# Unit 0's q and k through GpSimd's queue as bf16, turned without a copy

## The chip, the core and the metric

The kernel runs on one core of a Trainium2 chip. A core has TensorE (PE in the profile, PEld its weight loads), VectorE (DVE), ScalarE (ACT), GpSimd (POOL) and SyncE (SP), and sixteen DMA engines that move data between device memory and the on-chip memory. Every engine works through its own instruction list in order; semaphores make one wait for another. The metric is the device time of one execution in microseconds (us). Loads can be issued by SP and ACT (hardware_dynamic queues in the profile) or by GpSimd (software_dynamic queue); only the loads that GpSimd issues change the type on the way, here from float32 to bf16.

## The reference

Attention, then a two-layer block with a leaky ReLU, on float32 inputs:

```python
# q, k, v: (8, 12, 448, 64); w_in: (768, 2048); w_out: (2048, 768)
scores = np.matmul(q, k.transpose(0, 1, 3, 2)) / 8
attn = softmax(scores)                       # over the keys
x = np.matmul(attn, v)                       # heads side by side: (3584, 768)
h = x @ w_in
out = np.maximum(0.01 * h, h) @ w_out        # (3584, 768)
```

## The kernel before, in words

**Units.** A unit is a pair of heads of one batch entry, so there are 48, six to a batch entry. For a unit q and k come in as rows (112 partitions, four rows of 64 to a partition and head), are turned by TensorE or by a DMA transpose into `qkT` (128 partitions: the two heads' 64 components), and give scores in four chunks of 112 keys (`scores`, L331). ScalarE takes the exponential of each chunk from PSUM (`expo`, L349 to L351), TensorE multiplies it with v (`pv`, L360, and `rows`, L866), and VectorE divides by the sums (reciprocal L375 or L899, product L376 or L900) to give x, which is turned again and fed to the two-layer block in steps of 384 to 640 rows. Both layers use seven products in place of eight per pair of blocks; sums of weight blocks for this are made on VectorE (`mix_w_in`, L454, and `mix_weights`, L435).

**Order.** The schedule is written out by hand. Each engine executes in the order in which the code names its instructions; for the later stages a small model of due times (`place`, L973) chooses that order while the program is built. GpSimd's loads wait for the eighth load before them, so that at most eight are on their way.

**The start (L226 to L286).** SP and ACT load k and q of unit 0 as float32 (224 KB each), then k and q of unit 1; SP then loads v of unit 0. GpSimd makes the identity for the transposes, and then copies one column of unit 0's q (L234), which makes it wait for that load, before it issues its own loads: unit 2's q and k, v of units 1 and 2, unit 3's q and k, and so on (`load_soft`, L167). TensorE multiplies constants 39 times (`warm_up`, L271). VectorE clears small edges of tiles. ScalarE loads its table of functions behind its two load issues (L252). Then `both` (L281) casts k and q of unit 0 to bf16 in `qkb`, one head on ScalarE and one on VectorE.

**The first turn (`transposes`, L306).** For unit 0, k is turned first and q second, each by four transposes of 112 x 128 (both heads side by side), a few multiplications by zeros (`stay_warm`, L265: 3 behind k, 5 behind q), and a copy out of PSUM (k on ScalarE, q on VectorE, L320). The scores of unit 0 follow. Unit 1's k and q are cast on VectorE (L796) and turned behind the third chunk of unit 0.

**The second place (`neck`, L703).** While the first layer's columns beyond the head are made (L716), VectorE makes the sums of w_out's quarters, step by step, where `after` (L722) says: its tuple gives the number of steps after each of the eight groups. There are two rounds of six sums (L442, L444, L447); the second round needs the last of w_out's four loads. In between stand the reciprocal and product of a unit's x (L899, L900), which free a PSUM slot of TensorE's scores. Behind the sums stand four subtractions in w_out itself (L451). The second layer (`block_pair`, L604) follows: after its first product VectorE subtracts blocks of h (L633) and copies the result out of PSUM (`keep`, L626), and the third product uses the summed weights `w_mix`.

Of the kernel before, what the change touches and what calls it, by code (L numbers as in the profile page):

```python
# [16 lines left out]
def kernel(  # L17
# [13 lines left out]
    P = 128  # L31
# [135 lines left out]
    def load_soft(u, n, which):  # L167
        b, hp = divmod(u, HP)
        for x in which:
            if x > 0 and u >= WIDE:  # L170
                load_wide(u, x)
                continue
            t = room(x)
            nc.gpsimd.dma_start(
                out=half(t)[:, :n].rearrange("p u h so d -> p (u h) (so d)"),
                in_=(q, k, v)[x][b, 2 * hp:2 * hp + 2 * n].rearrange(
                    "h (p so) d -> p h (so d)", so=NSC),
            )
            for i in range(n):
                raw.setdefault(u + i, {})[x] = half(t, i)  # L180

    def load_one(u, x, queue):
        b, hp = divmod(u, HP)
        t = room(x)[:SC]
        queue.dma_start(
            out=t.rearrange("p h so d -> p h (so d)"),
            in_=(q, k, v)[x][b, 2 * hp:2 * hp + 2].rearrange("h (p so) d -> p h (so d)", so=NSC),
        )
        raw.setdefault(u, {})[x] = t
# [33 lines left out]
                o, i = w_steps.pop(0)  # L223
                nc.gpsimd.dma_start(out=o, in_=i)  # L224

    load_one(0, 1, nc.sync)  # L226
    load_one(0, 0, nc.scalar)
    load_one(1, 1, nc.sync)
    load_one(1, 0, nc.scalar)
    early = c_pool.tile([P, 4 * P], F32, name="c")  # L230
    ident = early[:, :P // 2].bitcast(BF16)
    make_identity(nc, ident)
    load_one(0, 2, nc.sync)
    nc.gpsimd.tensor_copy(early[:SC, P // 2 + 2:P // 2 + 3], raw[0][0][:, 0, 0, :1])  # L234
    load_soft(2, 1, (0, 1))
    load_soft(1, 2, (2,))
    load_soft(3, 1, (0, 1))
    cast(0, (2,))
# [8 lines left out]
    nc.vector.memset(warm[:, :P], 0.0)  # L247
    nc.vector.memset(warm[:, P:], 0.0)

    gate = early[:, P // 2:P // 2 + 2]  # L250
    nc.vector.memset(gate, 0.0)
    nc.scalar.copy(gate[:, :1], gate[:, 1:])  # L252

    ones = nc.const_aps.tensor(1.0, [P, P], BF16)

# [12 lines left out]
        for _ in range(n):  # L268
            nc.tensor.matmul(ps[:, 0, :P], warm[:, :P], warm[:, :P], start=True, stop=True)

    warm_up(39)  # L271
    for t in v_sb:
        nc.vector.memset(t[:, :, :, D:D + 1], 1.0)
    for t in e_sb:
# [2 lines left out]
    for t in qkT:  # L277
        nc.vector.memset(t[:, QL:QL + P - SC], 0.0)
    fast = nc.vector.tensor_copy

    def both(o, i):  # L281
        nc.scalar.copy(o[:, 0], i[:, 0])
        fast(o[:, 1], i[:, 1])

    cast(0, (1,), both)
    cast(0, (0,), both)  # L286


    x_t = {}
# [16 lines left out]
    def transposes(u, bank=None):  # L306
        if u >= min(NPE, NU):
            return
        gone.add(u)
        for parts in ((1,), (0,)) if u == 0 else ((0, 1),):  # L310
            tr = turn_tile(bank)
            for i in parts:
                for so in range(NSC):
                    nc.tensor.transpose(
                        tr[:, i, ts(so, SC)], qk_sb[u][:SC, i * NSC + so], ident[:SC, :SC]
                    )
            if u == 0:
                stay_warm(3 if parts == (1,) else 5)
            at = slice(parts[0], parts[-1] + 1)
            (nc.scalar.copy if u == NPE - 1 or u == 0 and parts == (1,) else nc.vector.tensor_copy)(  # L320
                qkT[u % NQ][:, :QL].rearrange("p (i s) -> p i s", i=2)[:, at], tr[:, at]
            )
# [281 lines left out]
    def block_pair(i, c):  # L604

        lo, hi = slice(0, MH), slice(MH, MD)
        x1, x2 = spots(i)[1][c]
        one, two = ts(x1, P), ts(x2, P)
        s3 = h_mix[:, :, c]
        t2, t3, t4 = (w_mix[:, x] for x in range(3))  # L610
        t1 = w_out_sb[:, lo, NW:]
        left, right = slice(0, NW), slice(NW, DM)
        o1 = o_pool.tile([P, DM], F32, name="o")
        o2 = o_pool.tile([P, DM], F32, name="o")
        b, a = banks

        def product(ps, x, w, first=False, cols=slice(0, NW)):
            for m in range(MH):
                if m in (2, 4, 6):
                    yield  # L620
                nc.tensor.matmul(  # L621
                    ps[:, cols], x[:, m], w[:, m], start=(first and m == 0), stop=(m == MH - 1), skip_group_check=True,
                )

        def keep(o, at, ps, by=nc.vector.tensor_copy):
            by(o[:, at], ps[:, :NW])  # L626

        def join(o, at, ps):
            nc.vector.tensor_add(o[:, at], o[:, at], ps[:, :NW])  # L629

        yield
        yield from product(b, h[:, lo, one], w_out_sb[:, lo, left], first=True)
        nc.vector.tensor_sub(h[:, lo, one], h[:, lo, two], h[:, lo, one])  # L633
        short = cuts[i + 1] - cuts[i] < 4 * P
        keep(o1, left, b, nc.scalar.copy if c == 0 and (short or i + 1 == NR) else nc.vector.tensor_copy)
        yield
        yield from product(a, h[:, hi, one], w_out_sb[:, hi, left], first=True)
        join(o1, left, a)
        nc.vector.tensor_sub(h[:, hi, one], h[:, hi, one], h[:, lo, one])
        yield  # L640
        yield from product(b, h[:, lo, one], t2)
        keep(o1, right, b)
        yield
        yield from product(a, h[:, lo, two], t1, first=True)
        keep(o2, right, a)
        yield
        yield from product(b, s3, t3)
        join(o2, right, b)
        yield
        t0 = token(i, x2)  # L650
        last = t0 + P == B * S
        if last:
            nc.vector.tensor_copy(o2[:, 2 * P:NW], b[:, 2 * P:NW])
            store(o1, token(i, x1), left)
            store(o2, t0, right)
        yield from product(a, h[:, hi, one], w_out_sb[:, hi, right])
        join(o1, right, a)
        if last:
            store(o1, token(i, x1), right, (nc.sync, nc.scalar))
        else:  # L660
            store(o1, token(i, x1))
        yield
        if last:
            w1, w2 = slice(0, 2 * P), slice(2 * P, NW)
            yield from product(b, h[:, hi, two], t4[:, :, w1], cols=w1)
            nc.vector.tensor_copy(o2[:, w1], b[:, w1])
            store(o2, t0, w1, (nc.scalar, nc.sync))
            end = slots[0][:, 0]
            yield from product(end, h[:, hi, two], t4[:, :, w2], first=True, cols=w2)
            nc.vector.tensor_add(o2[:, w2], o2[:, w2], end[:, w2])  # L670
            store(o2, t0, w2, (nc.sync, nc.scalar))
            return
        yield from product(b, h[:, hi, two], t4)
        keep(o2, left, b)
        store(o2, t0)
        banks.reverse()

    known = slice(0, HEAD - 3 * P)
# [24 lines left out]
    def neck(outs):  # L703

        n = cuts[1] - HEAD
        at = place_of(HEAD)
        ms = [x + y for x in range(0, MH, 2) for y in (0, MH)]
        held = {}

        def part2(m, kks):  # L710
            fresh = m not in held
            if fresh:
                held[m] = next_bank()
            for j in range(2):
                for kk in kks:
                    nc.tensor.matmul(  # L716
                        held[m][:, j * n:(j + 1) * n], w_in_sb[:, kk, ts(m + j, P)], xT[:, kk, at:at + n],
                        start=(fresh and j == 0 and kk == 0), stop=(kk == KD - 1), skip_group_check=True,
                    )

        assert all(u == need[1] - 1 for u, _ in owed_x), owed_x
        def after(x):  # L722
            for _ in range((0, 0, 2, 3, 4, 3, 0, 3)[x]):
                next(outs)

        for m in ms[:2]:
            part2(m, range(KD - 1))
        yield 4 * (KD - 1) * n / 2400, False
        for x, m in enumerate(ms):
            if x < 2:  # L730
                assert rows_done >= need[1], rows_done
                settle_x()
                part2(m, (KD - 1,))
                if x:
                    after(x - 1)
            else:
                part2(m, range(KH))
                after(x - 1)
                yield 2 * KH * n / 2400, False
                part2(m, range(KH, KD))  # L740
            nc.scalar.activation(
                h[:, m:m + 2, HEAD:cuts[1]], held.pop(m)[:, :2 * n].rearrange("p (m t) -> p m t", m=2), AX.Prelu, alpha=0.01
            )
            if x < 2:
                mix_first(4 * x, 1, known)
                mix_first(4 * x + 2, 1, known)
            settle(1)
            yield 2 * (KH if x > 1 else 1) * n / 2400, True
        model["free"][id(slots[0])] = model["now"] + 1.5
        transposes(NPE - 1, next_slot()[:, 0])  # L750
        after(len(ms) - 1)
# [388 lines left out]
```

## Time and profile before

| | |
|---|---|
| time, median of 3 runs | 380.48 us (380.31 to 380.56) |
| time of the profiled execution | 382.25 us |
| its span, first to last instruction | 380.1 us |
| PE busy | 372.1 us (98%) |
| ACT busy | 253.1 us (67%) |
| VectorE busy | 232.6 us (61%) |
| GpSimd busy | 153.4 us (40%) |
| first load of k landed, issued at 0.76 | 4.34 us |
| first load of q landed, issued at 0.76 | 4.70 us |
| GpSimd's first load issue | 5.00 us |
| first scores on PE | 6.66 us |
| first exponential on ACT | 7.06 us |
| last quarter of w_out landed | 70.90 us |

Times within the execution count from the start of the span. A line of a timeline reads: start, length, engine, line of the kernel, operation, output<-input, shapes, and xN for N such instructions together; in brackets stands how long the engine was idle before and what ended that. A line L12 is line 12 of the kernel; a helper's line stands for all its callers. Matmuls are pipelined, so one's length is longer than the distance to the next (its pitch). A DMA's time to landing counts from its issue.

### The profile page before, as it was taken

Reading aid. Unit: us, or ns where it says so; the run is one execution under the profiler, and the core shown is the slowest. Engines: PE = TensorE matmul, PEld = TensorE weight load, DVE = VectorE, ACT = ScalarE, POOL = GpSimd, SP = SyncE. Lnnn points to the kernel's source line nnn. Section 1 sums busy time; section 2 is a strip of 40 time slices with the busy share of each in tenths; the row PEclk is TensorE's granted clock in tenths of the full one; section 3 lists DMA queues with packets and bytes.
Section 4 is the critical chain, followed back from the end, with each engine's and each line's share of the span. In section 5 each row is a group of like instructions: output and inputs, shape, how many; then the busy total and the mean of one; then the engine's idle time right before and its main releaser. Section 6 shows DMA issues by size and latency. Waiting matters only on the chain.

```text
span 380.1 us, 9894 instructions
## 1 busy us (share of the span) xinstructions
PE 372.1 (98%) x3969; PEld 261.9 (69%) x3969; DVE 232.6 (61%) x512; ACT 253.1 (67%) x392; POOL 153.4 (40%) x302
## 2 busy tenths in 40 slices
PE   9899999899999999999999999999999999999995
PEld 7665658655598565896558975589755896668753
DVE  3662767687566655568475674655746566574753
ACT  5997895765777867677684786846867478318600
POOL 5866654397434934337333383334463000000000
PEclk9999999999999999999999999999999999999999
DMA  8999999999889997999957999679997550330022
GB/s 161 176 197 203 196 158 204 179 129 191 111 172 110 99 155 143 145 139 103 140 106 139 141 104 117 128 120 146 88 126 148 123 84 0 109 84 14 0 85 84
DMA packets 107678, 48.07 MB, mean 126 GB/s; under 512 B 79728, under 2 KB 104304, under 8 KB 107632
## 3 DMA queue, kind: packets, MB, share of 16 engines
q0 software_dynamic: 48096, 22.24, 51.1%
q1 hardware_dynamic: 58800, 24.54, 35.3%
q10 hardware_dynamic: 736, 0.66, 0.6%
q8 instruction: 31, 0.51, 0.6%
q14 instruction: 15, 0.12, 0.1%
HBM read 45.61 MB, written 11.01 MB: 149 GB/s over the span
## 4 chain that ended last, share of the span: by engine, by line
PE 78%; DMA 16%; POOL 3%; DVE 2%; issue 1%; POOLq 0%; DVEq 0%
PE g L621 34%; PE g L549 14%; PE sc L549 14%; PE sc L337 6%; DMA w_out_sb<-in_moe_w_out_dram 6%; PE sc L888 6%; DMA fq<-in_q_dram 4%; DMA w_mix<-in_v_dram 3%; PE sc L893 2%; PE sc L356 2%; DMA w_in_mix<-in_v_dram 1%; PE sc L877 1%; DMA hmix<-in_q_dram 1%; POOL w_in_sb L224 0%; POOL qkb L209 0%
## 5 line engine op out<-in xcount | busy, mean ns | idle before, releaser
L351 ACT ACTIVATE e<-sc 128x896 bf16<-128x896 f32 (+1 forms) x162 | 137.5, 922 | 43.5 <-PE sc L337 43.3
L621 PEld LDWEIGHTS <-h 128*128 128x128 bf16 x680 | 62.8, 98 | 50.1 <-issue 12.9
L621 PE MATMUL g<-w_out_sb,h 128*128 128x384 bf16 x448 | 86.4, 327 | 0.1
L538 ACT ACTIVATE h<-c 128x512 bf16<-128x512 f32 (+1 forms) x72 | 43.7, 611 | 28.2 <-DVE c L564 13.3
L549 PEld LDWEIGHTS <-w_in_sb 128*128 128x128 bf16 x576 | 54.6, 98 | 6.2
L337 PE MATMUL sc<-qkT 64*128 64x448 bf16 x324 | 42.5, 353 | 2.8 <-DVE x L900 1.4
L626 DVE COPY o<-g 128x384 f32<-128x384 f32 x53 | 29.4, 555 | 25.1 <-PE g L621 24.9
L549 PEld LDWEIGHTS <-w_in_mix 128*128 128x128 bf16 x432 | 41.0, 98 | 4.0
L209 POOL COPY v<-fv 128x256 f32<-128x256 f32 (+1 forms) x38 | 16.1, 433 | 67.7 <-PE sc L893 47.0
L621 PE MATMUL g<-w_mix,h 128*128 128x384 bf16 (+1 forms) x224 | 41.9, 325 | 0.0
L629 DVE TENSOR_TENSOR o<-o,g 128x384 f32<-128x384 f32 x42 | 23.2, 552 | 19.6 <-PE g L621 17.7
L888 PEld LDWEIGHTS <-e 128*128 128x128 bf16 x720 | 30.4, 97 | 3.5 <-ACT e L351 2.4
L888 PE MATMUL sc<-v,e 128*128 128x65 bf16 x720 | 32.1, 193 | 0.0
L209 POOL COPY qkb<-fq 112x256 f32<-112x256 f32 x38 | 16.7, 440 | 37.9 <-DMA qkT<-qkb 19.4
L900 DVE TENSOR_TENSOR x<-sc,rec 112x512 bf16<-112x512 f32 x42 | 29.0, 692 | 1.5
L337 PEld LDWEIGHTS <-qkT 64*128 64x128 bf16 x324 | 12.5, 94 | 25.1 <-issue 18.1
L549 PE MATMUL g<-xT,w_in_sb 128*128 128x256 bf16 (+1 forms) x216 | 28.5, 268 | 0.0
L549 PE MATMUL sc<-xT,w_in_sb 128*128 128x256 bf16 (+1 forms) x216 | 28.5, 268 | 0.0
L899 DVE RECIPROCAL rec<-sc 112x8 f32<-112x8 f32 x42 | 8.7, 207 | 29.5 <-PE sc L893 14.2
L893 PE MATMUL sc<-v,e 128*128 128x130 bf16 x120 | 26.7, 223 | 0.0
L209 POOL COPY qkb<-fk 128x256 f32<-128x256 f32 (+1 forms) x38 | 18.7, 492 | 19.0 <-DMA fk<-in_k_dram 17.9
L621 PE MATMUL g<-w_mix,hmix 128*128 128x384 bf16 x112 | 23.1, 326 | 0.0
(123 smaller groups left out, 589.5 us busy)
## 6 DMA issues: line engine op xcount, KB each, us to landing
fq<-in_q_dram POOLq DMA_DIRECT2D x19, 224.0 KB, 5.9
w_in_sb<-in_moe_w_in_dram POOLq DMA_DIRECT2D x4, 768.0 KB, 12.6
w_out_sb<-in_moe_w_out_dram POOLq DMA_DIRECT2D x4, 768.0 KB, 19.6
fk<-in_k_dram POOLq DMA_DIRECT2D x15, 192.0 KB, 5.7
fv<-in_v_dram POOLq DMA_DIRECT2D x15, 192.0 KB, 4.2
out_dram<-o SPq DMA_DIRECT2D x7, 336.0 KB, 3.6
out_dram<-o SPq DMA_DIRECT2D x8, 288.0 KB, 3.4
out_dram<-o SPq DMA_DIRECT2D x7, 240.0 KB, 3.1
```

Source lines behind the costliest of these rows:

```text
L209: by(t.rearrange("p so h d -> p h so d") if x < 2 else t[:, :, :, :d], f)
L337: nc.tensor.matmul(ps[:, j, :S], t[j * D:(j + 1) * D, k0:k0 + P], q_of(u)[j * D:(j + 1) * D] if u >= WIDE else t[j * D:(j + 1) * D, :S], s ...
L351: nc.scalar.activation(e[:, :, c, :], sc_t.pop((u, c))[:e.shape[0], :, :S], AX.Exp, scale=scale)
L538: nc.scalar.activation(hs[:, m:m + 2, cols], x.rearrange("p (m t) -> p m t", m=2), AX.Prelu, alpha=0.01)
L549: nc.tensor.matmul(ps[:, j * nh:(j + 1) * nh], w[:, kk, ts(j, P)], x[:, kk], start=(first and j == 0 and kk == 0), stop=(kk == KH - 1), sk ...
L621: nc.tensor.matmul(ps[:, cols], x[:, m], w[:, m], start=(first and m == 0), stop=(m == MH - 1), skip_group_check=True,)
L626: by(o[:, at], ps[:, :NW])
L629: nc.vector.tensor_add(o[:, at], o[:, at], ps[:, :NW])
L888: nc.tensor.matmul(ps[:, b, y + j, :D + 1], e[:, at:at + P], vt[:, j, c, :D + 1], start=(y + j + c == 0), stop=False, skip_group_check=True,)
L893: nc.tensor.matmul(ps[:, b, y:y + 2, :D + 1], e[:, at:at + P], vt[:, :, NWC, :D + 1], start=False, stop=True, skip_group_check=True,)
L899: nc.vector.reciprocal(rec, ps[:SC, :, :, D:D + 1])
L900: nc.vector.tensor_mul(x, ps[:SC, :, :, :D], rec.to_broadcast([SC, 2, NSC, D]))
```

## The change

Unit 0's k and q are loaded by GpSimd, as its first two instructions, as bf16. The transposes read the loaded rows directly: each head of each row group on its own (112 x 64), eight per tensor, into the upper or lower 64 partitions of PSUM. The casts of unit 0 and GpSimd's touch of q go. SP now loads only unit 1's k; unit 1's q and unit 0's v are issued by ACT, behind its table load, which moves ahead with the small memset that it reads. The warm-up goes from 39 to 29 multiplications, those behind k from 3 to 0 and behind q from 5 to 6. In `after` the counts for groups 4 to 6 go from 4, 3, 0 to 3, 0, 4, so that the six sums of the second round are split: two before, and four behind, the reciprocal and product of a unit's x. The order of all other instructions on the engines stays; `queues` in `block_pair` is given its default.

```diff
-    load_one(0, 1, nc.sync)
-    load_one(0, 0, nc.scalar)
+    load_soft(0, 1, (1, 0))
     load_one(1, 1, nc.sync)
-    load_one(1, 0, nc.scalar)
     early = c_pool.tile([P, 4 * P], F32, name="c")
+    gate = early[:, P // 2:P // 2 + 2]
+    nc.vector.memset(gate, 0.0)
+    nc.scalar.copy(gate[:, :1], gate[:, 1:])
     ident = early[:, :P // 2].bitcast(BF16)
     make_identity(nc, ident)
-    load_one(0, 2, nc.sync)
-    nc.gpsimd.tensor_copy(early[:SC, P // 2 + 2:P // 2 + 3], raw[0][0][:, 0, 0, :1])
     load_soft(2, 1, (0, 1))
+    load_one(1, 0, nc.scalar)
+    load_one(0, 2, nc.scalar)
     load_soft(1, 2, (2,))
...
-    gate = early[:, P // 2:P // 2 + 2]
-    nc.vector.memset(gate, 0.0)
-    nc.scalar.copy(gate[:, :1], gate[:, 1:])
...
-    warm_up(39)
+    warm_up(29)
...
-    def both(o, i):
-        nc.scalar.copy(o[:, 0], i[:, 0])
-        fast(o[:, 1], i[:, 1])
-
-    cast(0, (1,), both)
-    cast(0, (0,), both)
...
                 for so in range(NSC):
+                    if u == 0:
+                        for j in range(2):
+                            nc.tensor.transpose(tr[j * D:(j + 1) * D, i, ts(so, SC)], raw[0][i][:, j, so], ident[:SC, :SC])
+                        continue
                     nc.tensor.transpose(
                         tr[:, i, ts(so, SC)], qk_sb[u][:SC, i * NSC + so], ident[:SC, :SC]
                     )
             if u == 0:
-                stay_warm(3 if parts == (1,) else 5)
+                stay_warm(0 if parts == (1,) else 6)
...
-        store(o2, t0)
+        store(o2, t0, queues=(nc.sync, nc.sync))
...
-            for _ in range((0, 0, 2, 3, 4, 3, 0, 3)[x]):
+            for _ in range((0, 0, 2, 3, 3, 0, 4, 3)[x]):
```

## The prediction

> **What bounds the kernel now.** I read the page's busy times first, then the chain that ended last, then the waits stage by stage, then the timelines of the two places that the change touches. PE is busy for 98% of the span:
>
> ```profile
> PE 372.1 (98%) x3969; PEld 261.9 (69%) x3969; DVE 232.6 (61%) x512; ACT 253.1 (67%) x392; POOL 153.4 (40%) x302
> ```
>
> This is a mean over stages with different limits. The first is ScalarE's (its timeline, 0 to 40 us):
>
> ```profile
> 5.52 0.53 ACT L320 COPY qkT<-g 128x448 bf16<-128x448 bf16 x1 [0.40 <-PE g L314]
> 7.06 19.61 ACT L351 ACTIVATE e<-sc 112x896 bf16<-112x896 f32 x24 [1.01 <-PE sc L337]
> 27.12 2.53 ACT L351 ACTIVATE e<-sc 112x896 bf16<-112x896 f32 x3 [0.44 <-PE sc L337]
> ```
>
> 24 exponentials run without a pause from 7.06 to 26.67, 0.82 us each, so whatever moves the first one moves the stage. From 26 us PE is full, with one hole. The chain of waits from 0 to 80 us, whose columns are start, length and what, shows it behind a transfer:
>
> ```profile
> 48.38 22.53 DMA w_out_sb<-in_moe_w_out_dram
> ...
> 71.00 0.57 DVE w_mix L442
> ...
> 74.50 0.70 DVE x L900
> 75.20 0.04 issue
> 75.24 0.56 PE sc L337 x4
> ```
>
> The timelines of PE and VectorE show the same place from both sides:
>
> ```profile
> 73.48 0.36 PE L337 MATMUL sc<-qkT 64*128 64x448 bf16 x2
> 75.24 0.56 PE L337 MATMUL sc<-qkT 64*128 64x448 bf16 x4 [1.40 <-DVE x L900]
> ```
>
> ```profile
> 71.00 0.56 DVE L442 TENSOR_TENSOR w_mix<-w_out_sb 128x768 bf16<-128x768 bf16 x1 [3.31 <-DMA w_out_sb<-in_moe_w_out_dram]
> ...
> 73.13 1.22 DVE L447 TENSOR_TENSOR w_mix<-w_out_sb,w_mix 128x768 bf16<-128x768 bf16 x2
> 74.27 0.19 DVE L899 RECIPROCAL rec<-sc 112x8 f32<-112x8 f32 x1
> 74.50 0.69 DVE L900 TENSOR_TENSOR x<-sc,rec 112x512 bf16<-112x512 f32 x1
> ```
>
> VectorE waits 3.31 us for the last quarter of w_out (landed 70.90), does six sums for the weights, and only then empties the PSUM slot that PE filled by 71.5. PE stands 1.40 us for it. From 80 to 300 us it is idle for 0.1 us in all, so what PE wins here should reach the end.
>
> **Edit 1, the order on VectorE (tuple in `after`).** The counts of steps go from 2, 3, 4, 3, 0, 3 to 2, 3, 3, 0, 4, 3 (positions 2 to 7). In the changed order the reciprocal and x stand behind two of the six sums, not behind all six. With w_out at 70.90 again, the sums start at 71.00 and 71.59, the reciprocal at 72.06 (where the third sum was) and x at 72.29, done at 72.98. PE reaches its scores at 73.84: no stall, **1.40 us won**, 0.86 us to spare. What is late next: the four other sums take 2.21 us (72.06 to 74.27 before), so from 72.90 to 75.11; two of L451 follow as before to 76.12, the subtraction of L633 (pitch 0.61) to 76.73, the copy L626 (0.55) to 77.28. PE's first product with w_mix needs that copy, ran at 78.67, and now comes at 77.27. So this edit alone fits to 0.01 us, and what is won earlier passes only as far as w_out lands earlier too.
>
> **Edit 2, the start.** It removes two ScalarE casts (0.40 each), two VectorE casts (0.29 each) and GpSimd's touch of q (0.31), and ten warm-up matmuls (39 took 4.08 us of weight loads, so 29 end near 3.8). It adds two load issues on GpSimd and eight transposes. Before, q landed at 4.70 and the scores started at 6.66, 1.96 us later.
>
> Landing. The only rows of GpSimd loads of this size on an empty queue are unit 2's q and k (DMA issues; KB each, us to landing):
>
> ```profile
> hmix<-in_q_dram ACTq DMA_DIRECT2D x1, 224.0 KB, 3.9
> hmix<-in_k_dram SPq DMA_DIRECT2D x1, 224.0 KB, 3.6
> w_in_mix<-in_q_dram POOLq DMA_DIRECT2D x1, 112.0 KB, 3.0
> w_in_mix<-in_k_dram POOLq DMA_DIRECT2D x1, 112.0 KB, 3.0
> ```
>
> Issued at 0.75 (0.80 us) and 1.55 (0.66 us), k lands at 3.75 and q at 4.55 if nothing collides. But k of unit 1 goes out on SP at 0.76, and q of unit 1 on ACT at about 2.3 (table load 1.28, copy 0.19, then the issue), so its packets mix with q0's. By 5.0 us the trace of before had moved 881 packets from five loads; k0, q0, k1 (224 each) and 200 of q1 are 872. With equal shares q0's last packet is thus near 5.0 and it lands (0.5 later, as unit 2's q did) at 5.5. I take the middle, **5.0**, between 4.55 and 5.5.
>
> By the Trainium skill, DMA: Bandwidth & Descriptors (Specifications), the first byte takes about 1 us on GpSimd's path and 0.6 on SP's or ACT's, which speaks against the move. Here SP's first packets came 1.0 us after issue and GpSimd's 1.4, so the row has the same 0.4. The 3.0 us above holds it already; with the page's 1 us the sum would be at most 0.4 better.
>
> Turning. Before, four transposes of q took 0.58 from first start to last end, at a pitch of 0.10. Eight half-wide ones are not in this trace: one after the other 0.30 + 7 x 0.10 = 1.0; two at a time, as the 64-row scores ran (six in 0.74), 0.6. I take 0.8. Then VectorE's copy, 0.39, and 0.15 of hand-overs: 5.0 + 0.1 + 0.8 + 0.54 = 6.44 against 6.66, **0.2 won**. The ends are 4.55 with 0.6 (5.79: 0.9 won) and 5.5 with 1.0 (7.14: 0.5 lost). The six stay-warm matmuls (0.64) lie beside the copy. k's half is ready by then: landed at 3.75 to 4.3, eight transposes, ScalarE's copy 0.53, done by 5.9.
>
> Hidden: the identity now stands behind two issues on GpSimd (done near 2.8, before k lands). q1 lands between 5.9 and 7.4 (2.3 plus 3.6 to 5.1); its cast starts about 6.8, and the fourth chunk of scores behind it has 1.2 us before ScalarE asks (ran at 8.27, wanted at 9.5). v0, issued near 2.75 plus 5.2, lands by 8.0; GpSimd's cast of it ran at 8.51, and its first reader at 10.75. Behind that cast wait GpSimd's next load issues; the queue ahead of them is not empty by then, since two of its first seven loads go out only between 5.0 and 6.4.
>
> **The transfers.** Unit 2's loads go out near 2.8, not 5.0. The queue is full from 7 to 70.9 (the weights' last DMA took 22.53 us from issue), so this is worth only the hole that it closes. This row of DMA busy tenths is 6 to 10 us in 40 slices:
>
> ```profile
> DMA  7520099625999999999999958979989999999999
> ```
>
> The first ten slices hold about half their worth: 0.5 us. I take w_out **0.5 earlier** (0, if the queue's rate is the limit anyway, to 1.0).
>
> **The sum.** 1.40 from the order on VectorE, 0.20 from the start, let through by 0.5 of w_out: 1.6 us. The profiled execution took 382.25 us (span 380.1 and 2.15 around it) and would take 380.65. The median of the timed runs is 380.48, 1.77 below that execution, so I carry the difference over: **378.9 us**. With the ends: 1.40 + 0.9 = 2.3 won at best (378.2), 1.40 - 0.5 = 0.9 at worst (379.6).
>
> **Rivals.**
> *q0 late beyond that.* GpSimd's first loads share the engines with two queues, and 5.5 is a guess of equal shares; at 6.0 with serial turning the scores start at 7.64, 1.0 late. Then 0.4 is won: 380.1. For it: 4.70 was reached by loads that started 0.4 us earlier. Against: two loads stood beside q0's there too.
> *The stall comes back.* PE arrives 1.6 us earlier at the next transfers: after 70 us GpSimd waited 1.4 us for a load of v and 1.0 for one of k, and their times hang on the full queue. If PE then waits for them or for w_mix, between 0 and 0.6 of the gain is left: about 380.2. Against: PE shows no wait for a DMA there now.
> *PE stays slow: slower.* Its matmuls of 128 columns kept a pitch of 0.105 to 6.4 us, and transposes of 112 columns one of 0.10 until then and 0.05 after. The start now has ten fewer warm-ups and eight more transposes. A unit in ScalarE's stage costs PE about 2.5 us of its 3.27 (four pairs of scores 0.76, eight transposes 0.41, two products with v 1.1, four turns of x 0.2, by the pitches of the timeline); at half pace 5.0. Each slow microsecond behind the first scores loses 0.35 us (1.7 of 5.0), so from 4.6 us of it the whole gain of 1.6 is gone, and at 6.8 us it is 0.8 slower: 381.3. For it: the switch came only at 6.4, close to the scores. Against: PE keeps working without a gap over 0.4 us.
> The Trainium skill, TensorE: Matmul & The Clock Gate (What's actually happening), has the gate watch windows of about 3.4 us, and Part 4 says that transposes don't count as busy the same way; by that, swapping warm-ups for transposes is what could miss a window. The trace agrees on the two paces and cannot show what counts.
>
> **Chances.** Forecast 0.60 (378.2 to 379.6); q0 late 0.15; the stall back 0.11; PE slow 0.14. 0.2% is 0.76 us, about what a measurement of this kernel can tell from no change; within it I put the second rival, most of the first, and nothing of the forecast: faster 0.66, same 0.20, slower 0.14. The range, 378.1 to 380.9, takes in forecast and the first two rivals and leaves out the slow one and the far ends.
>
> **What would show it.** First exponential near 6.85 (7.06 before). No wait of PE for x near 73; the reciprocal between the second and third sum; the DMA wait of VectorE ending near 70.4. The hole in the DMA row at 6 us gone. I am wrong if the first exponential comes after 7.6, if weight loads still take 147 ns behind the scores, or if the 1.4 us stand again at another instruction before 80 us.

## The result: 382.34 us, and the profile after

The changed kernel takes 382.34 us (median of 5 runs, 381.58 to 383.47), the kernel before 380.31 in the runs beside it: a ratio of 1.0052 [1.0034, 1.0071], so 2.0 us slower. Forecast was 378.9. The profiled execution after took 383.47 us (span 381.5), 1.1 above its median. Ratios and their intervals leave out an execution that is more than 1.5% above the fastest of its kernel; only `ident_first` has such executions, two of them.

ScalarE's timeline after, start and length first (lines of code are five lower than before):

```profile
0.74 1.28 ACT L231 ACT_TABLE_LOAD   x1 [0.74 <-PEq L1119]
0.92 0.40 ACTq L185 DMA_DIRECT2D w_in_mix<-in_q_dram  x1
1.36 0.47 ACTq L185 DMA_DIRECT2D w_in_mix<-in_v_dram  x1
...
6.74 0.53 ACT L315 COPY qkT<-g 128x448 bf16<-128x448 bf16 x1 [4.51 <-PE g L307]
8.19 2.53 ACT L346 ACTIVATE e<-sc 112x896 bf16<-112x896 f32 x3 [0.91 <-PE sc L332]
11.09 0.92 ACT L346 ACTIVATE e<-sc 112x896 bf16<-112x896 f32 x1 [0.37 <-PE sc L332]
12.16 16.38 ACT L346 ACTIVATE e<-sc 112x896 bf16<-112x896 f32 x20 [0.15 <-PE sc L332]
```

The first exponential comes at 8.19 (7.06 before), and the 24 no longer run without a pause: there are gaps of 0.37 and 0.15 where ScalarE waits for scores. They end at 28.54, 1.87 later than before (26.67). The first three lines hold the surprise: ACT's two loads go out at 0.92 and 1.36, while the table load is still running and before the copy (2.04) that the code names ahead of them.

GpSimd's first instructions after:

```profile
1.31 0.79 POOL L174 DMA_DIRECT2D hmix<-in_k_dram  x1 [0.85 <-POOLq L1119]
2.08 0.68 POOL L174 DMA_DIRECT2D hmix<-in_q_dram  x1
```

and the DMA issues of the first 20 us after (KB each, us from issue to landing):

```profile
w_in_mix<-in_k_dram SPq DMA_DIRECT2D x1, 224.0 KB, 3.0
w_in_mix<-in_q_dram ACTq DMA_DIRECT2D x1, 224.0 KB, 3.7
w_in_mix<-in_v_dram ACTq DMA_DIRECT2D x1, 224.0 KB, 4.4
...
hmix<-in_k_dram POOLq DMA_DIRECT2D x1, 112.0 KB, 5.0
hmix<-in_q_dram POOLq DMA_DIRECT2D x1, 112.0 KB, 4.8
```

So k of unit 0 lands at 1.31 + 5.0 = 6.3 and q at 2.08 + 4.8 = 6.9, behind unit 1's q (0.92 + 3.7 = 4.6) and unit 0's v (1.36 + 4.4 = 5.8), which are wanted much later. The queues between 2.5 and 3.9 us show who was served (q10 is ACT's, q1 SP's, q0 GpSimd's):

```profile
q10 hardware_dynamic: 342, 0.33, 78.1%
q1 hardware_dynamic: 100, 0.09, 21.2%
q0 software_dynamic: 1, 0.00, 0.3%
```

One packet of GpSimd's in 1.4 us. TensorE meanwhile ran out of work (its timeline after):

```profile
0.79 3.25 PE L256 MATMUL g<-const-bfloat16-1.0 128*128 128x128 bf16 x29 [0.79 <-PEq L1119]
6.31 0.39 PE L307 MATMUL g<-c,hmix 112*64 112x112 bf16 x8 [2.27 <-DMA hmix<-in_k_dram]
6.91 0.39 PE L307 MATMUL g<-c,hmix 112*64 112x112 bf16 x8 [0.21 <-DMA hmix<-in_q_dram]
7.23 0.51 PE L267 MATMUL sc<-x_mix 128*128 128x128 bf16 x6
7.79 1.06 PE L332 MATMUL sc<-qkT 64*128 64x448 bf16 x6
```

It stands 2.27 us for k, turns k and q in 0.39 each, and slows down in the middle of the scores (six in 1.06, later 0.74). A table of stretches (length, PE busy, granted clock, DMA share, GB/s) has the reason:

```profile
6.30:8.10 1.80, 1.53 (x26) 0.99 1.29 167
8.10:11.50 3.40, 3.40 (x20) 0.50 1.29 164
11.50:15.00 3.50, 3.23 (x54) 1.00 1.33 165
```

For 3.4 us behind the idle time the granted clock is 0.50. By the Trainium skill, TensorE: Matmul & The Clock Gate (What's actually happening), the gate judges free-running windows of about 3.4 us and halves the clock after an idle one; the length of the slow stretch agrees. The idle time here, 2.27 us, is shorter than such a window, so this rule alone does not give the slow stretch; what the other executions say of it stands under *The clock*.

The second place, VectorE after:

```profile
69.28 0.55 DVE L437 TENSOR_TENSOR w_mix<-w_out_sb 128x768 bf16<-128x768 bf16 x1
69.87 0.56 DVE L439 TENSOR_TENSOR w_mix<-w_mix,w_out_sb 128x768 bf16<-128x768 bf16 x1
73.47 0.21 DVE L894 RECIPROCAL rec<-sc 112x8 f32<-112x8 f32 x1 [3.05 <-PE sc L872]
73.72 0.69 DVE L895 TENSOR_TENSOR x<-sc,rec 112x512 bf16<-112x512 f32 x1
74.33 0.55 DVE L437 TENSOR_TENSOR w_mix<-w_out_sb 128x768 bf16<-128x768 bf16 x1
74.91 0.56 DVE L439 TENSOR_TENSOR w_mix<-w_mix,w_out_sb 128x768 bf16<-128x768 bf16 x1
75.38 2.38 DVE L442 TENSOR_TENSOR w_mix<-w_out_sb,w_mix 128x768 bf16<-128x768 bf16 x2
77.69 1.21 DVE L446 TENSOR_TENSOR w_out_sb<-w_out_sb 128x768 bf16<-128x768 bf16 x2
78.82 0.88 DVE L628 TENSOR_TENSOR h<-h 128x1024 bf16<-128x1024 bf16 x1
79.62 0.55 DVE L621 COPY o<-g 128x384 f32<-128x384 f32 x1
```

No wait for w_out is left. VectorE waits 3.05 us for TensorE, then does x and the last four sums, and one pair of these takes 2.38 us (1.22 before). TensorE and GpSimd at that time:

```profile
75.34 0.78 PE L332 MATMUL sc<-qkT 64*128 64x448 bf16 x6
...
80.22 0.81 PE L616 MATMUL g<-w_mix,h 128*128 128x384 bf16 x4 [1.07 <-DVE o L621]
```

```profile
75.93 0.41 POOL L209 COPY v<-fv 112x256 f32<-112x256 f32 x1
76.27 0.41 POOL L209 COPY qkb<-fq 112x256 f32<-112x256 f32 x1
76.61 0.74 POOL L209 COPY qkb<-fk 112x256 f32<-112x256 f32 x1
```

The hole for x is gone (six scores in a row at 75.34), but the first product with w_mix, wanted at 79.15, waits 1.07 us for the copy L621. Behind it TensorE has no wait over 0.05 us in either kernel.

### The profile page after: what moved, and what is told of

Same layout as the page of the kernel before. It is cut to its first block, busy times and chain, and to the rows that moved or that the text cites. A ratio compares the mean times of both kernels' runs of the same rounds, so it can differ in the third digit from the quotient of the medians.

```text
span 381.5 us, 9877 instructions
## 1 busy us (share of the span) xinstructions
PE 372.0 (98%) x3965; PEld 260.9 (68%) x3965; DVE 232.4 (61%) x510; ACT 252.4 (66%) x390; POOL 156.3 (41%) x303
## 4 chain that ended last, share of the span: by engine, by line
PE 92%; DVE 2%; ACT 2%; issue 2%; DMA 1%; POOL 0%; DVEq 0%; POOLq 0%
PE g L616 33%; PE g L544 14%; PE sc L544 14%; PE sc L332 9%; PE sc L883 6%; PE g L425 4%; PE sc L872 3%; PE g L711 2%; PE sc L888 2%; ACT e L346 2%; PE sc L351 1%; DMA hmix<-in_q_dram 1%; PE g L309 1%; PE g L363 1%; PE sc L425 1%
## 5 line engine op out<-in xcount | busy, mean ns | idle before, releaser
L209 POOL COPY v<-fv 128x256 f32<-128x256 f32 (+1 forms) x38 | 14.9, 401 | 75.0 <-PE sc L888 47.5
L621 DVE COPY o<-g 128x384 f32<-128x384 f32 x53 | 29.4, 555 | 25.1 <-PE g L616 25.0
L209 POOL COPY qkb<-fq 112x256 f32<-112x256 f32 x38 | 18.5, 486 | 41.9 <-DMA fq<-in_q_dram 19.7
L209 POOL COPY qkb<-fk 128x256 f32<-128x256 f32 (+1 forms) x38 | 19.9, 524 | 14.7 <-DMA fk<-in_k_dram 14.0
```

Of the source, the lines that this page charges most:

```text
L209: by(t.rearrange("p so h d -> p h so d") if x < 2 else t[:, :, :, :d], f)
```

## The experiments

The theory after the traces, before any experiment: unit 0's k and q come late because ACT's loads are served first; TensorE's idle time then costs a slow window; the new order then has no hole for x left to close, and only moves four sums next to GpSimd's copies. Rivals: GpSimd's path is that slow by itself; the slow clock costs nothing in the end; the new order does win its 1.40 us and the start loses 3.4. In the expectations "A" is the theory as it stood then.

**Each half alone.** `start_only`: the changed kernel with the old tuple.

```diff
-            for _ in range((0, 0, 2, 3, 3, 0, 4, 3)[x]):
+            for _ in range((0, 0, 2, 3, 4, 3, 0, 3)[x]):
```

> The change's start with the old counts of steps on VectorE. Theory A (both halves of the change cost or give nothing; the start loses about 1.9 us by 28 us, and the new order only pushes four sums into GpSimd's copies): first exponential near 8.2 and the first 24 ending near 28.5 as in the changed kernel, w_out landing near 68.4, the six sums done by 72.5, no wait of PE for VectorE between 73 and 81, and the whole 0.5 to 1.1 us faster than the changed kernel, so 0.9 to 1.5 us slower than the kernel before. Theory B (the new order is worth its 1.4 us and only the start loses): PE waits again near 75 and the kernel is 3 us or more slower than the one before.

Measured: 381.81 us, ratio 1.0032 [1.0019, 1.0045]. TensorE's only wait in the second place, from its timeline:

```profile
80.93 0.36 PE L332 MATMUL sc<-qkT 64*128 64x448 bf16 x2 [0.33 <-DVE x L895]
```

With the changed start the old order leaves a hole of 0.33, the new one 1.07. There is no wait for x near 75: with its stage 2.2 us later (24th exponential at 28.84) TensorE comes later to the slot, and w_out is here sooner (the six sums began at 69.77, at 71.00 before), so that VectorE is done in time. So the late start takes most of the hole away, and costs less than the 2.2 us by which its stage is late. (How much less can't be added up from this one execution: at 382.72 us it is 0.9 above its median.)

`order_only`: the kernel before with the new tuple (the reverse of the edit above).

> The start of the kernel before with the new counts of steps on VectorE. Theory A (the four sums that are left until the last hit GpSimd's copies and stall PE ahead of the product with w_mix): the wait for x near 73.8 is gone, a wait of 0.5 to 1.3 us stands ahead of that product, and the time is within 0.8 us of the kernel before. Theory B (my prediction's first edit): 1.0 to 1.4 us faster than the kernel before, with no wait of PE over 0.3 us between 73 and 81.

Measured: 380.44 us, ratio 0.9996 [0.9986, 1.0007], no change. VectorE waits 1.82 us for w_out and goes on at 68.78; TensorE's one wait:

```profile
79.31 1.46 PE L621 MATMUL g<-w_out_sb,h 128*128 128x384 bf16 x8 [0.34 <-DVE o L629]
```

Theory A's wait comes at another product, and is shorter than its 0.5 to 1.3 us.

The start loses 1.5 us, the new order wins nothing that the times show, and on top of the new start it costs about 0.5 (382.34 less 381.81; the two intervals overlap, so the profile's 1.07 against 0.33 has to carry this).

**Why did order_only win nothing?** The kernel before, unchanged, profiled again, and the new order too.

> The kernel before, unchanged, profiled once more. Theory A (the 1.40 us hole of TensorE at 73.84 was a feature of one slow execution: its span was 380.1 us, that of most timed runs is 378.2): the last quarter of w_out lands near 68.7, not at 70.90, x is done by 72.6, TensorE stands for it under 0.4 us, the first exponential is between 6.5 and 7.1, the execution takes 380.0 to 380.8 us. Rival B (the hole is there in every execution and the new order does win it, but gives it back elsewhere): w_out lands near 70.9 and TensorE stands 1.2 to 1.5 us for x again.

> The kernel before, profiled a third time. The profiles so far fit one sum: span = 371.3 (within 0.4) + start of the first exponential with the gaps of its stage + TensorE's holes between 60 and 82 us. Theory A (the hole for x depends on when w_out lands, which differs by up to 2 us between executions of the same program): w_out lands anywhere between 68.5 and 71, the hole is that landing less 69.2, none below, and the span follows the sum within 0.4 us. Rival B (the order of VectorE's work itself moves w_out): w_out lands at 70 us or later again and the hole is 1.0 to 1.5 us.

> The kernel before with the new order alone, profiled a second time. Theory A (w_out's landing varies by execution; the new order takes the hole away wherever it lands): no wait for x above 0.1 us, another wait of 0 to 0.5 us between 76 and 82 us, span 371.3 plus the first exponential plus that wait, within 0.4. Rival B (the order moves w_out): it lands at 68.5 to 69.0 again.

Measured: 381.01, 380.32 and 380.03 us. The hole of the kernel before in the two executions, `again` first:

```profile
74.50 0.56 PE L337 MATMUL sc<-qkT 64*128 64x448 bf16 x4 [1.09 <-DVE x L900]
```

```profile
73.81 0.56 PE L337 MATMUL sc<-qkT 64*128 64x448 bf16 x4 [0.52 <-DVE x L900]
```

The first speaks against theory A of its expectation, that the hole belongs to one late execution; the second, whose time is near the median, shows 0.52 us, where the rule in its own expectation gives under 0.4. VectorE could go on with w_out at 71.00, 70.26 and 69.56 in the three profiles of before, and the holes are 1.40, 1.09 and 0.52. With the new order it was 68.78 and 69.22, and 0.34 and 0.35 of hole at another instruction. So w_out's landing differs by over 1 us between executions of one program; the new order takes the hole for x away, and gives back 0.35. It can win 1.05 in a late execution and 0.2 in a median one, and 0.2 is not to be seen in the times.

Rival B, that the order itself moves w_out, has no way to act: in the traces of both orders every engine executes the same instructions in the same order until w_out has landed, and the first that differs is the third that VectorE executes behind it. Yet in each of the three starts the executions with the new order have w_out sooner than those with the old one (with the start of before, GpSimd's next load, which waits for it, goes out at 68.97 and 69.41 against 69.75 to 71.19). What sorts them was not settled.

**The collision.** `held`: ACT's two loads wait until unit 0's q has landed, as VectorE writes one number of it to their destinations first (its memsets are moved ahead of that).

```diff
+    for x in (0, 2):
+        nc.vector.tensor_copy(rooms[0][:SC, 0, 0, :1] if x == 0 else rooms[1][:SC, 0, 0, :1], raw[0][0][:, 0, 0, :1])
     load_one(1, 0, nc.scalar)
     load_one(0, 2, nc.scalar)
```

> The changed kernel with ACT's loads of unit 1's q and unit 0's v held back until unit 0's q has landed: VectorE copies one number of q into each of their destinations, and the loads wait for that. Theory A (GpSimd's first loads are late because ACT's loads stand beside them): first packets of GpSimd's queue 1.4 us after issue and not 2.5, k landing 3.0 to 3.5 us after issue (near 4.6 in place of 6.3), q near 5.2 in place of 6.9. Theory B (GpSimd's first load is slow by itself): k lands 4.5 us or more after issue, as in the changed kernel. In both, v of unit 0 lands later, GpSimd's later loads go out later, and the whole may be slower; the landing times decide.

`all_soft`: unit 1's k and q and unit 0's v by GpSimd as well, behind unit 0's.

```diff
-    load_one(1, 1, nc.sync)
...
-    load_soft(2, 1, (0, 1))
-    load_one(1, 0, nc.scalar)
-    load_one(0, 2, nc.scalar)
+    load_soft(1, 1, (1, 0))
+    load_soft(0, 1, (2,))
+    load_soft(2, 1, (0, 1))
```

> The changed kernel with unit 1's k and q and unit 0's v loaded as bf16 by GpSimd too, behind unit 0's and the identity, so that no other queue's packets are ahead of unit 0's. Theory A (k and q of unit 0 came late because 672 KB of SP's and ACT's loads went first): k lands at 4.2 to 4.8 and q at 4.9 to 5.5 (3.0 to 3.4 us after issues at 1.31 and 2.08), not at 6.3 and 6.9; the first exponential comes at 6.6 to 7.1 instead of 8.19; with unit 1's operands in time the median is 380.3 to 381.3. Rival B (GpSimd's path itself takes 4.8 us here): k and q land at 6.0 or later as before, the first exponential stays at 8 us, and the median at 382 or above. What could hide A: unit 1's loads, issued behind, are late by up to 1 us.

Unit 0's loads, `held` first, then `all_soft`:

```profile
hmix<-in_k_dram POOLq DMA_DIRECT2D x1, 112.0 KB, 3.4
hmix<-in_q_dram POOLq DMA_DIRECT2D x1, 112.0 KB, 3.3
```

```profile
hmix<-in_k_dram POOLq DMA_DIRECT2D x1, 112.0 KB, 3.1
hmix<-in_q_dram POOLq DMA_DIRECT2D x1, 112.0 KB, 3.3
```

With the issues still at 1.31 and 2.08, both loads are 1.5 to 1.9 us faster without ACT's packets. SP's load of unit 1's k stood beside them in `held` and did no such harm. GpSimd's path is not slow by itself. Two things stay open: whether it is ACT's queue or simply 448 KB more ahead that does the harm, and whether GpSimd's packets stood in line or were not yet there to be served. In `all_soft` the first exponential is back at 6.66:

```profile
6.66 19.61 ACT L345 ACTIVATE e<-sc 112x896 bf16<-112x896 f32 x24 [1.13 <-PE sc L331]
```

and the time is 380.96 us, ratio 1.0010 [0.9992, 1.0028]: what the start lost is given back, but nothing is won. Here too the new order costs a hole, 0.85 us at 78.87. `held` as a whole is much slower, 386.35 us, 1.0149 [1.0129, 1.0169]: unit 1's q now comes behind GpSimd's full queue, and ScalarE waits 3.49 us for its scores. So these loads can't simply wait.

**The clock.** `warm`: the changed kernel with 52 warm-up multiplications in place of 29, which last until k is there. `start_warm`: the same with the old tuple.

```diff
-    warm_up(29)
+    warm_up(52)
```

> The changed kernel with 52 warm-up matmuls in place of 29, so that PE does not stand idle for 2.3 us ahead of the first transposes. Theory A (the idle time puts PE on its slow pace from 8.1 to 11.5, and ScalarE runs dry for it): first exponential still near 8.0, no idle time of ScalarE between the first 24, their end near 27.7 in place of 28.54, and 0.5 to 0.9 us faster than the changed kernel. Theory B (ScalarE's gaps come from the late loads of unit 1): the gaps stay, and the time is within 0.3 us of the changed kernel.

> The changed start with the old order of the sums and 52 warm-up multiplications instead of 29. Theory A (the start costs 1.5 us, of which the slow clock behind TensorE's idle time costs 0.6 to 0.8, and the new order costs 0.5 on top): median 380.9 to 381.3, 0.5 to 0.9 below the start alone (381.81). Rival B (the slow clock costs nothing in the end, since transfers set the pace behind it): 381.6 to 382.0.

Measured: 381.73 us, 1.0043 [1.0028, 1.0057], and 381.15 us, 1.0012 [1.0001, 1.0024]; that is 0.6 below the changed kernel and 0.7 below `start_only` by the medians, 0.3 and 0.8 by the ratios. In `warm`:

```profile
8.09 19.62 ACT L346 ACTIVATE e<-sc 112x896 bf16<-112x896 f32 x24 [0.71 <-PE sc L332]
```

```profile
8.10:11.50 3.40, 2.65 (x23) 1.00 1.38 183
```

The clock is whole between 8.1 and 11.5 us, the gaps are gone, and the stage ends at 27.71 instead of 28.54. Each pair alone overlaps in its intervals; two pairs and the profile say the same.

This does not show that the idle time is what costs the clock, because `warm` ends the idle time and also gives TensorE 23 more products. Two executions with 29 of them are slow from the first transposes on: `start_only`, behind 2.23 us of idle time, and `soft_old` (further below), where none is over 0.36 us. `start_only` first:

```profile
6.27 0.96 PE L307 MATMUL g<-c,hmix 112*64 112x112 bf16 x16 [2.23 <-DMA hmix<-in_k_dram]
7.91 1.30 PE L332 MATMUL sc<-qkT 64*128 64x448 bf16 x6
```

```profile
6.52 1.30 PE L331 MATMUL sc<-qkT 64*128 64x448 bf16 x6
```

Six scores take 0.74 us at the full clock. The clock column reads 1.00 at these places, but it does so wherever the trace has no record of the clock yet, and the first record, of a full clock, stands at 11.7 us in `start_only` and at 9.2 in `soft_old`. With 29 warm-up multiplications it stands at 4.0 to 18.5 us in seven executions; two of these lose the full clock again for 3.4 us (`after` and `ident_first`), and only one, `all_soft`, has it through the scores of unit 0. With 39 or 52 it stands at 3.8 to 6.6 us in seven executions, and all keep it. So the slow scores go with the shorter warm-up, with a long idle time behind it or without; how the two share the blame in `after` stays open.

**The copies.** `no_copies`: four of GpSimd's copies near 76 us are left out.

```diff
+            if by == nc.gpsimd.tensor_copy and casts[0] in (43, 44, 45, 46):
+                continue
```

> The changed kernel without four of GpSimd's copies (a v, a q and a k, and another q; they ran at 75.93, 76.27, 76.61 and 77.99 in the changed kernel's profile), so that units' attention there is computed from old values. Theory A (VectorE's sum of two inputs took 1.71 us in place of 0.55 because GpSimd's copies ran beside it): the sum at 75.9 takes 0.55 to 0.7, the copy that the w_mix product waits for is 0.8 to 1.2 us earlier against the x before it, the wait of TensorE at that product (1.07 us) falls below 0.3, and the median is 0.5 to 1.0 us below the changed kernel's 382.34, 381.3 to 381.8. Rival B (the sum was long for another reason, such as a transfer or a semaphore): it takes 1.5 us or more again, the wait stays near 1 us, and the median stays at 382.0 to 382.6.

Measured: 381.69 us, 1.0037 [1.0023, 1.0050], 0.65 below the changed kernel, whose interval overlaps. The pair of sums in this kernel:

```profile
75.05 1.02 DVE L447 TENSOR_TENSOR w_mix<-w_out_sb,w_mix 128x768 bf16<-128x768 bf16 x2
```

1.02 us instead of 2.38, and TensorE has no hole left between 60 and 82 us. The Trainium skill, SBUF — State Buffer (section "SBUF: two separate sides"), says that VectorE and GpSimd share a pair of ports that one of them holds for a whole instruction, a VectorE operation on two inputs from SBUF against a GpSimd one that reads SBUF; these runs agree, with 1.36 us for three copies in a row.

**Is there a version that beats both?** `soft_old`: `all_soft` with the old tuple. `ident_first`: that with the identity ahead of GpSimd's first loads.

```diff
-    load_soft(0, 1, (1, 0))
...
     make_identity(nc, ident)
+    load_soft(0, 1, (1, 0))
```

> All of the first loads by GpSimd (as in the run all_soft) with the old order of the sums. In all_soft x was free at 72.1 without a wait, but TensorE stood 0.85 us at 78.87 for the next x, behind a subtraction of VectorE that took 1.43 us beside GpSimd's copies. Theory A (which order loses less is a matter of whose copies the sums run beside): with the old order the hole is 0.3 to 0.9 us at either place, first exponential 6.6 to 6.8, median 380.1 to 380.9, the same as before. Rival B (the new order costs 0.5 us wherever w_out is early): 380.2 to 380.5, and the spread of all_soft (379.33 to 382.98) shrinks.

> As soft_old, with the identity in front of GpSimd's first loads. Theory A (GpSimd can't issue its first load before 1.31 us whatever stands ahead, since its queue was busy until then): the identity (0.75 to 1.32) costs the first issue nothing, k lands at 4.3 to 4.5 and q at 5.2 to 5.4, unit 1's loads go out 0.55 us earlier, first exponential 6.5 to 6.7, median equal to soft_old's or up to 0.3 below. Rival B (the first issue of a load needs 0.85 us of its own behind whatever is ahead): first issue at 1.85 to 2.2, first exponential 7.1 to 7.3, 0.5 us above soft_old.

Measured: 381.07 us, 1.0014 [1.0001, 1.0027], and 382.29 us, 1.0040 [1.0015, 1.0065] with single runs from 379.84 to 385.66. Both expectations are missed. In `soft_old` k and q landed as early as in `all_soft`, but TensorE was slow when it turned them (0.58 and 0.59 us for eight in place of 0.51 and 0.39), and the first exponential came at 7.11. In `ident_first` GpSimd's first load goes out at 1.52, so the identity in front costs 0.21, not nothing and not its whole 0.57; q then took 3.6 us, TensorE lost the full clock from 7.4 to 10.9 us, and ScalarE had a gap of 0.41. What scatters its times by 5 us was not settled. No version beat the kernel before.

**One sum for all.** The end of ScalarE's 24 exponentials and TensorE's hole in the second place (73 to 84 us) account for every profiled execution; what is left of the span is 351.3 to 352.0 us. All figures are in us.

| execution | 24th ends | hole | span | rest |
|---|---|---|---|---|
| before | 26.67 | 1.40 | 380.1 | 352.0 |
| again | 26.24 | 1.09 | 378.9 | 351.6 |
| again2 | 26.11 | 0.52 | 378.2 | 351.6 |
| order_only | 26.13 | 0.34 | 378.3 | 351.8 |
| order2 | 25.90 | 0.35 | 377.9 | 351.7 |
| all_soft | 26.27 | 0.85 | 378.9 | 351.8 |
| soft_old | 27.01 | 0.54 | 379.2 | 351.6 |
| ident_first | 27.54 | 0.79 | 380.1 | 351.8 |
| start_warm | 27.62 | 0.33 | 379.4 | 351.5 |
| warm | 27.71 | 0.19 | 379.8 | 351.9 |
| no_copies | 28.21 | 0.00 | 379.5 | 351.3 |
| after | 28.54 | 1.07 | 381.5 | 351.9 |
| start_only | 28.84 | 0.33 | 380.7 | 351.5 |
| held | 32.47 | 0.40 | 384.4 | 351.5 |

Against `again2`, the execution of before at its median, the changed kernel's loses 2.4 us in the stage and 0.55 in the hole. That is more than the 2.0 us of the medians because this execution is 1.1 above its own.

## Why the prediction was wrong

*What bounds the kernel* was read rightly: the first exponentials and the hole near 74 us are the two places that count, and what comes later differs by 0.7 us at most.

*Edit 2, the landing, is the step that failed.* Three numbers in it. GpSimd's issue was put at 0.75, where its memset ran before; it was 1.31. ACT's loads were put at 2.3, "behind the table load", because the code names them there; they went out at 0.92 and 1.36. And the packets were shared out equally, with 3.0 us to landing from loads that GpSimd had issued later; with ACT's packets waiting, GpSimd got one packet in 1.4 us, and the loads took 5.0 and 4.8. Without ACT's loads they take 2.9 to 3.6, near what the row said. Together q landed at 6.9, not 5.0. The rival *q0 late beyond that* had the mechanism and a far bound (6.0) that was 0.9 too early. A small reading is off too: in the trace of before GpSimd's first packets came 1.5 us after the issue, not 1.4, and ACT's, which the prediction does not give, 1.4.

*The turning* was cheaper than both ends: 0.39 us for eight where 0.6 to 1.0 were allowed (0.58 where TensorE was slow, in `soft_old`). It could not make up for 1.9.

*PE stays slow* was a rival at 0.14 and came true. By the price of its row, 0.35 us for each of 3.4 slow microseconds, it costs 1.2; the profile shows 0.7 in the stage (28.54 less 8.19 and 19.61), and 52 warm-up multiplications won 0.6. The argument against it, that TensorE has no gap over 0.4 us, failed twice: with q at 6.9 the gap was 2.27, and in `soft_old`, where q was early and no gap was over 0.36, TensorE was slow all the same. What was said for it held: the full clock came only just before the scores even with 39 warm-up multiplications (6.6 us in the execution that was read), and ten of them were taken away. Six of the seven executions with 29 were slow within the scores of unit 0. So this does not come with a late q alone.

*Edit 1* removed the hole for x as worked out, and the point where it would come back was named: the w_mix product that "fits to 0.01 us". With no room the durations had to hold, and a pair of sums took 2.38 us beside GpSimd's copies where 1.22 was counted; the copies were not looked at. How much comes back hangs on where the copies fall: in `warm`, with the same order, the pair took 1.49 and the hole was 0.19. So 1.07 of the 1.40 came back, where the old order leaves 0.33 (`start_only`). The signs named for a wrong prediction were there: a first exponential after 7.6, a slow clock behind the scores, and a stall at another instruction from 79.15 us on.

*The transfers*: w_out was taken 0.5 earlier. GpSimd, whose next load waits for it, goes on at 67.86 to 70.03 in the five executions with the changed start (`after`, `start_only`, `warm`, `start_warm`, `no_copies`), and at 68.97 to 71.19 in the five with the old start. Since the executions with the new order are the earlier ones in both, they are compared within one order: there the changed start is 0.8 to 0.9 earlier on the mean, inside the 0 to 1.0 that was allowed. With that, and with TensorE late, the start alone does what edit 1 is for, and the two could not add up.

*The sum*: 1.40 us was taken from an execution 1.77 us above the median, and the difference was then carried over as if it were something else. Half of that lateness was the hole itself (1.40 against 0.52 in `again2`), a third the stage (26.67 against 26.11). At most 0.5 was to be won there, 0.2 with what the new order gives back. The 3.4 us between forecast and measurement are then 2.1 in the stage (28.54 against 26.47, of which 0.7 are the gaps), 1.1 in the hole, and 0.6 for a lateness of 1.77 carried over in full where the changed kernel's profile was 1.1 late, less 0.3 in the rest and around the span.

## What to carry to other kernels

Don't take a load's place in the code for its time of issue (here two went out before the copy named ahead of them): check in a trace whether the instructions ahead really hold it, and which queue's packets are served while two wait. A hole behind a transfer is worth what it is in the median execution, so profile twice before counting it, and never subtract a profile's whole lateness and its cause both. Read TensorE's clock from the pace of its products, and not from the clock column alone. Where a reordered step fits "to 0.01 us", look at what the neighbouring engine does at that moment before calling it a fit.

## What the runs showed of the hardware

- ACT's queue issued two loads (0.92, 1.36 us) while ACT_TABLE_LOAD ran (0.74 to 2.02), before the copy named ahead of them (2.04).
- While ACT's queue moved 342 packets in 1.4 us, GpSimd's moved 1 (0 in `start_only`, `warm` and `start_warm`); without ACT's loads 214 beside 91 of SP's (`held`) and 279 alone (`all_soft`) in the same 1.4 us.
- GpSimd's first load issue came at 1.31 us with no instruction of the kernel's own code ahead and at 1.52 behind 0.57 us of identity.
- With 29 warm-up multiplications TensorE's full clock was first granted at 4.0 to 18.5 us, and twice lost again for 3.4 us (`after`, `ident_first`); with 39 or 52 it was granted at 3.8 to 6.6 us, and kept (seven executions each).
- The clock column reads 1.00 where the trace has no record yet, also while six scores take 1.30 us instead of 0.74 (`start_only`, 7.91 us).
- Eight transposes of 112 x 64, into two halves of the partitions, took 0.39 us at the full clock, as long as four of 112 x 128 (0.37 in `again`).
- w_out's landing, near 70 us, moved by 1.4 us between three executions of one program.
